# One pair's rotated keys taken from TensorE to GpSimd and DMAs, and the next pair's keys split before its queries, in an attention and mixture-of-experts kernel

## The chip, the cores and the metric

The kernel runs on one core of one Trainium2 chip. The metric is the device time of one execution in microseconds (us); of several runs the median is taken.

## What is computed

Attention with rotary embeddings over 4 batches, 8 heads, 576 tokens and a head width of 64, followed by a mixture of experts with one expert per token. The experts take most of the time after about 290 us and aren't touched here. The part that matters, cut:

```python
def rotate(x):
    x1, x2 = (x[..., :half], x[..., half:])
    return np.concatenate([x1 * cos - x2 * sin, x1 * sin + x2 * cos], axis=-1)
q_rot, k_rot = (rotate(q), rotate(k))
scores = scale * np.matmul(q_rot, k_rot.transpose(0, 1, 3, 2))
scores = scores - np.max(scores, axis=-1, keepdims=True)
attn = np.exp(scores)
attn = attn / (np.sum(attn, axis=-1, keepdims=True) + 1e-09)
return np.matmul(attn, v).astype(np.float32)
...
logits = np.einsum('bsd,de->bse', x, w_gate)
...
h = np.maximum(x[b, s] @ w1[e], 0.0)
out[b, s] = p[e] * (h @ w2[e])
```

## The kernel before

Two heads make a pair; there are 16 pairs, numbered from 0. A pair is nine tiles of 128 query rows against 576 keys (eight of one head each, and a tail tile of both heads' last 64 rows), so attention is 144 steps, g = 0 to 143. Up to g = 126 the order on every engine is the order of the code (a manual schedule).

Every number that goes through TensorE is a high part (fp32r) and the rest. In step g VectorE has the minimum mn of tile g (`softmax_min`, L278; the scores are negated, so the minimum is the maximum); TensorE makes the scores s of tile g+1 (`mm_s`, L273); ScalarE makes the exponentials e of tile g (`softmax_exp`, L295); VectorE takes the minimum of g+1; TensorE turns tile g-2 (`tr_main`, tm, L332), ScalarE copies it as its high part pth (`split_to`, L310) and VectorE makes the rest ptl (L314). Every fourth tile adds the narrow pieces tk, pkh, pkl. From g = 11 on the products with v follow (`pv_mm`, L371), ten steps behind. The scores have two PSUM buffers (pool ps_s): s of tile g+1 waits for the exponentials of tile g-1.

A pair's rotated queries and keys come in three ways.

- The usual way, from pair 2 on: SP loads four 128x576 pieces (queries, queries of the other half, keys, keys of the other half); GpSimd multiplies them by the table `tab` and adds two and two into `rr` (`rope_half`, L200 and L201), and splits rr into high part and rest in xq or xk (`split_qk`, L212 and L213). SP then spreads these with SBUF-to-SBUF DMAs: the tail queries (`spread_tail`, 2 DMAs), the queries (`spread_q`, 4) and the keys (`spread_k`, 6, to a tile m of the pool m_p, which has two buffers).
- Pair 0 (`first_pair`): VectorE and GpSimd make products with the table, and TensorE multiplies them by a 0/1 matrix `sel` (`turned`, L1144), which adds the two halves and puts them into both halves of the rows. ScalarE takes the high part from PSUM, VectorE the rest.
- Pair 1: the same, with products on GpSimd into the tile `raw`. `pair_1` (L1219) lists eight pieces: four `half_keys` of 288 columns (L1152 on ScalarE, L1155 on VectorE) and four `queries` of 256 or 320 columns (L1178 and L1184). The table START (L1246) puts them behind the steps 3 to 7.

The first index of `raw` holds pair 1's four pieces, the second pair 2's, which GpSimd turns at L200 and L201 in `rope_2` (step 3). The pool pt_p has four buffers: raw, then pth and ptl of pair 0 and pth of pair 1; ptl of pair 1 takes raw's place. The host lays out pairs 0 and 1 for the way with `sel` (`_laid_out`, L1402).

Queues: SP issues nearly all DMAs in the order of the code; one that waits holds up those behind it. A DMA of SP or ScalarE also waits for the landing of the eighth one before it. Pair p's spread is issued at the first step of pair p-1 (L1303), behind it the next loads of queries and keys (L1319); GpSimd's splits stand at step 5 (L1325).

Of the kernel before, what the change touches and what calls it, by code (L numbers as in the profile page):

```python
# [10 lines left out]
F32 = mybir.dt.float32  # L11
F32R = mybir.dt.float32r
# [5 lines left out]
ALU = mybir.AluOpType  # L18
# [119 lines left out]
def tile_attention_moe(ctx, tc, qk, v, tabs, turn, consts, tri, wg, wts, out):  # L138
# [48 lines left out]
    def load_qk(p):  # L187
        for f in (1, 0):
            load_half(p, f)
# [19 lines left out]
    def split_qk(p):  # L209
        parts = [(xq, rr)] if p % 2 == 0 else [(xk[1], rr[:, 1]), (xq[:, :, 0], rr[:, 0])]  # L210
        for x, src in parts:
            pool.tensor_scalar(x[:, 0], src, 1.0, 1.0, op0=ALU.mult, op1=ALU.mult)  # L212
            pool.tensor_tensor(x[:, 1], src, x[:, 0].bitcast(F32), op=ALU.subtract)  # L213

    def split_v(p):
        v2 = v2_p.tile([P, 10, 2, D], F32R, tag="v2", name=f"v2_{p}")
        src = vl[p % 2]
        pool.tensor_scalar(v2[:, :, 0], src, 1.0, 1.0, op0=ALU.mult, op1=ALU.mult)
        pool.tensor_tensor(v2[:, :, 1], src, v2[:, :, 0].bitcast(F32), op=ALU.subtract)
        v2_t[p] = v2  # L220
# [890 lines left out]
    def first_pair():  # L1111
        nonlocal qtail0

        wake = pk_p.tile([P, S], F32R, tag="pk", name="wake").bitcast(BF16)[:, 0:512]
        sel = et_p.tile([P, S], F32, tag="et", name="turn")[:, 0:P]
        sp.dma_start(qkl[:, 2, 0:HALF], qk[0, 0, :, 2, 0:HALF])
        act.dma_start(tab[:, 2, 0:HALF], tabs[:, 2, 0:HALF])
        sp.dma_start(qkl[:, 2, HALF:], qk[0, 0, :, 2, HALF:])
        act.dma_start(tab[:, 2, HALF:], tabs[:, 2, HALF:])
        act.dma_start(sel, turn)  # L1120
        sp.dma_start(qkl[:, 0, 0:256], qk[0, 0, :, 0, 0:256])
        sp.dma_start(qkl[:, 3], qk[0, 0, :, 3])
        sp.dma_start(qkl[:, 1, 0:256], qk[0, 0, :, 1, 0:256])
        for x in range(2):
            sp.dma_start(qkl[:, x, 256:], qk[0, 0, :, x, 256:])
        m_t[0] = m_p.tile([P, 2, 2, S], F32R, tag="m", name="m_0")
        qtail0 = et_p.tile([P, S], F32R, tag="et", name="qtail0")[:, 0:4 * P].rearrange("p (n a s) -> p n a s", n=2, a=2)
        qtail0 = [qtail0[:, n] for n in range(2)]


        dve.memset(wake, 0.0)
        awake = ps_t.tile([P, 512], F32, tag="t", name="wake_ps")

        def keep_awake(n):
# [11 lines left out]
        def half_keys(a, h, p=1, wait=False):

            ps = ps_t.tile([P, 512], F32, tag="t", name=f"k{p}_{a}_{h}")
            for c, lo, n in (((0, 0, HALF),), ((0, HALF, HALF),), ((64, 0, 224), (0, 512, 64)), ((0, 224, HALF),))[2 * a + h]:
                turned(2 + a, ps[:, c:c + n], lo, n, raw[:, 0] if p else qkl)  # L1150
            hi, lo = (m_t[p][:, a, c, h * HALF:(h + 1) * HALF] for c in range(2))
            act.copy(hi, ps[:, 0:HALF])  # L1152

            def rest():
                dve.tensor_tensor(lo, ps[:, 0:HALF], hi.bitcast(F32), op=ALU.subtract)  # L1155

            return rest if wait else rest()

        def keys(a):
            ps = ps_s.tile([P, 2, 512], F32, tag="s", name=f"k_{a}")  # L1160
            for h, c, lo, n in (((0, 0, 0, HALF), (1, 0, HALF, HALF)), ((0, 64, 0, 224), (1, 0, 224, HALF), (0, 0, 512, 64)))[a]:
                turned(2 + a, ps[:, h, c:c + n], lo, n)
            hi, lo = (m_t[0][:, a, c].rearrange("p (h s) -> p h s", h=2) for c in range(2))
            act.copy(hi, ps[:, :, 0:HALF])

            def rest():
                dve.tensor_tensor(lo, ps[:, :, 0:HALF], hi.bitcast(F32), op=ALU.subtract)

            return rest

        def queries(a, lo, hi, p=0):
            ps = ps_t.tile([P, 512], F32, tag="t", name=f"q{p}_{a}_{lo}")
            turned(a, ps[:, 0:hi - lo], lo, hi - lo, raw[:, 0] if p else qkl)
            parts = []
            for c0, c1 in ((lo, min(hi, 512)), (512, hi)):
# [24 lines left out]
        for x in (2, 3, 0, 1):  # L1200
            sp.dma_start(raw[:, 0, x], qk[0, 1, :, x])
        for x in range(2):
            products(x, 256, S, pool)
        low_k = keys(0)
        products(0, 0, 256)
        keep_awake(1)
        products(3)
        products(1, 0, 256)
        low_k()
        queries(0, 0, 256)()  # L1210
        second = [half_keys(1, h, 0, True) for h in range(2)]
        second.append(queries(1, 0, 256))
        mm_s(0)
        for f in second[0:2]:
            f()
        for x in (2, 3, 0, 1):
            products(x, engine=pool, of=raw[:, 0])
        m_t[1] = m_p.tile([P, 2, 2, S], F32R, tag="m", name="m_1")
        pair_1 = [lambda a=a, h=h: half_keys(a, h) for a in range(2) for h in range(2)]  # L1219
        pair_1 += [lambda a=a, lo=lo, hi=hi: queries(a, lo, hi, 1)() for a in range(2) for lo, hi in ((0, 256), (256, S))]  # L1220
        return [second[2], lambda: queries(0, 256, S)(), lambda: queries(1, 256, S)()], keep_awake, pair_1

    if True:
# [4 lines left out]
            rest_q, keep_awake, pair_1 = first_pair()  # L1228
        sp.dma_start(wid, wg)
        load_v(0)  # L1230
        sp.dma_start(tab[:, 3], tabs[:, 3])
        sp.dma_start(raw[:, 1], qk[0, 2])
        sp.dma_start(tab[:, 0:2], tabs[:, 0:2])
        load_v(1)
# [3 lines left out]
        sp.dma_start(rows_d[0:1], zrow)  # L1238

        def rope_2():  # L1240
            for f in (1, 0):
                rope_half(pool, f, raw[:, 1, 2 * f:2 * f + 2])

        NSTEP = NPAIR * 9
        soon, todo, minima = [], [], {}
        START = {  # L1246
            0: [lambda: split_v(0)], 1: [rest_q[1], lambda: keep_awake(1)], 2: [rest_q[2], lambda: load_qk(3)],
            3: [pair_1[0], pair_1[1], rope_2, lambda: split_qk(2)], 4: [pair_1[2]], 5: pair_1[3:5],
            6: pair_1[5:6], 7: pair_1[6:8] + [lambda: split_v(1), lambda: load_v(2)],
            8: [lambda: spread(2)], 40: [lambda: act.copy(trib, trif)],  # L1250
        }


# [146 lines left out]


def _laid_out(q, k, v, moe_w_gate, moe_w_local, moe_w1, moe_w2):  # L1402
    def turned(x):
        t = x.reshape(B, NP, 2, S, 2, D // 2).transpose(0, 1, 2, 4, 5, 3)
        x = np.stack([t.reshape(B, NP, 2, D, S), t[:, :, :, ::-1].reshape(B, NP, 2, D, S)], axis=4)
        x[:, :, 1] = x[:, :, 1, :, ::-1].copy()

        for hp in range(2):
# [5 lines left out]
    qk = np.concatenate([turned(q), turned(k)], axis=3)  # L1414
# [40 lines left out]
```

## Time and profile before

| | us |
|---|---|
| median of 3 runs | 538.61 |
| the 3 runs | 536.79, 538.71, 538.61 |
| the profiled execution | 537.63 |
| its span in the profile | 535.7 |
| TensorE busy (PE) | 515.3 |
| VectorE busy (DVE) | 377.4 |
| ScalarE busy (ACT) | 345.3 |
| GpSimd busy (POOL) | 346.1 |

In the profile an engine's work is named by the line of the kernel, the operation, and the tiles written and read (out<-in). Times are us from the start of the span. SPq is SyncE's queue, on which DMAs are issued. "[1.08 <-DVE gm L470]" behind a row says how long the engine had been idle and what ended that. The table is of the whole span; what a change in one stretch is worth has to be read from that stretch.

### The profile page before, as it was taken

Reading aid. Unit: us, or ns where it says so; the run is one execution under the profiler, and the core shown is the slowest. Engines: PE = TensorE matmul, PEld = TensorE weight load, DVE = VectorE, ACT = ScalarE, POOL = GpSimd, SP = SyncE. Lnnn points to the kernel's source line nnn. Section 1 sums busy time; section 2 is a strip of 40 time slices with the busy share of each in tenths; the row PEclk is TensorE's granted clock in tenths of the full one; section 3 lists DMA queues with packets and bytes.
Section 4 is the critical chain, followed back from the end, with each engine's and each line's share of the span. In section 5 each row is a group of like instructions: output and inputs, shape, how many; then the busy total and the mean of one; then the engine's idle time right before and its main releaser. Section 6 shows DMA issues by size and latency. Waiting matters only on the chain.

```text
span 535.7 us, 10815 instructions
## 1 busy us (share of the span) xinstructions
PE 515.3 (96%) x3273; PEld 458.9 (86%) x3273; DVE 377.4 (70%) x690; ACT 345.3 (64%) x766; POOL 346.1 (65%) x290
## 2 busy tenths in 40 slices
PE   7989999999999999999999899999999999999992
PEld 4889999999999999998978688887888888888881
DVE  6999999999999999999998746446421745411540
ACT  3988999999999999998877323252533344523440
POOL 4999999999999999983898202255412554411331
PEclk9999999999999999999999999999999999999997
DMA  8658788988879878866167214653446586537440
GB/s 280 275 133 224 224 221 232 236 188 215 221 224 246 200 194 211 239 150 159 24 210 227 65 55 142 190 205 127 169 105 231 150 325 182 181 90 235 107 151 25
DMA packets 65481, 97.33 MB, mean 182 GB/s; under 512 B 28353, under 2 KB 39105, under 8 KB 65282
## 3 DMA queue, kind: packets, MB, share of 16 engines
q1 hardware_dynamic: 61938, 86.45, 57.1%
q0 software_dynamic: 3040, 9.71, 5.6%
q8 instruction: 28, 0.46, 0.4%
q14 instruction: 43, 0.35, 0.3%
q10 hardware_dynamic: 432, 0.36, 0.2%
HBM read 76.95 MB, written 12.86 MB: 168 GB/s over the span
## 4 chain that ended last, share of the span: by engine, by line
PE 80%; DVE 8%; issue 4%; ACT 3%; POOL 2%; DMA 1%; ACTq 0%; POOLq 0%; DVEq 0%
PE h L981 19%; PE o L1024 17%; PE pv L371 14%; PE s L273 13%; PE tm L332 9%; PE gx L457 3%; DVE mn L278 2%; PE th L1015 2%; DVE ptl L314 2%; PE tx L967 2%; ACT e L295 1%; PE tk L342 1%; DMA turn<-in_turn_dram 1%; ACT pth L310 1%; DVE w L926 1%
## 5 line engine op out<-in xcount | busy, mean ns | idle before, releaser
L1024 PE MATMUL o<-w,hs 128*128 128x512 f32 x456 | 113.1, 398 | 0.0
L278 DVE TENSOR_REDUCE mn<-s 128x1 f32<-128x576 f32 x144 | 107.1, 743 | 2.3 <-PE s L273 1.1
L981 PE MATMUL h<-w,xs 128*128 128x512 f32 x444 | 106.4, 393 | 1.3 <-DVE xs L314 1.0
L295 ACT ACTIVATE e<-s,mn 128x576 f32<-128x576 f32 x128 | 95.5, 746 | 15.2 <-DVE mn L278 12.6
L1030 POOL DMA_INDIRECT out_dram<-os,sidx x19 | 23.1, 1213 | 125.4 <-ACTq L932 83.7
L314 DVE TENSOR_TENSOR ptl<-tm,pth 128x512 fp32r<-128x512 f32 x139 | 95.4, 687 | 11.5 <-ACT pth L310 8.8
L273 PE MATMUL s<-m,qst 128*128 128x288 f32 x512 | 96.2, 310 | 4.1 <-ACT e L295 3.0
L981 PEld LDWEIGHTS h<-w,xs 128*128 128x128 f32 x444 | 82.5, 188 | 19.9 <-DVE w L926 1.5
L1024 PEld LDWEIGHTS o<-w,hs 128*128 128x128 f32 x456 | 83.1, 188 | 17.0 <-DVE hs L314 0.4
L310 ACT CAST pth<-tm 128x512 fp32r<-128x512 f32 x139 | 80.7, 581 | 6.8 <-PE tm L332 6.2
L273 PEld LDWEIGHTS s<-m,qst 128*128 128x128 f32 x512 | 74.1, 188 | 9.0 <-ACT e L295 5.1
L371 PE MATMUL pv<-pth,v 128*128 128x288 f32 x256 | 76.8, 315 | 0.6 <-DVE ptl L314 0.4
L332 PE MATMUL tm<-wid,e 128*128 128x128 f32 x512 | 77.1, 272 | 0.0
L371 PE MATMUL pv<-ptl,v 128*128 128x288 f32 x256 | 76.5, 314 | 0.2 <-POOL ptl L307 0.2
L200 POOL TENSOR_TENSOR stage<-stage 128x1152 f32<-128x1152 f32 x26 | 69.4, 2669 | 1.1 <-DMA stage<-in_qk_dram 1.1
L332 PEld LDWEIGHTS tm<-wid,e 128*128 128x128 f32 x512 | 62.1, 140 | 0.8 <-DVE ptl L314 0.4
L926 DVE TENSOR_TENSOR w<-stage,w 128x1024 fp32r<-128x1024 f32 x37 | 51.2, 1418 | 14.6 <-ACT w L923 9.7
L371 PEld LDWEIGHTS pv<-pth,v 128*128 128x128 f32 x256 | 48.3, 189 | 2.0 <-DVE ptl L314 0.7
L371 PEld LDWEIGHTS pv<-ptl,v 128*128 128x128 f32 x256 | 48.3, 189 | 0.5 <-POOL ptl L307 0.4
L314 DVE TENSOR_TENSOR xs<-tx,xs 128x512 fp32r<-128x512 f32 x19 | 13.1, 688 | 44.9 <-ACTq L932 35.0
L201 POOL TENSOR_TENSOR stage<-stage 128x576 f32<-128x576 f32 x26 | 37.1, 1427 | 2.0
L314 DVE TENSOR_TENSOR hs<-th,hs 128x512 fp32r<-128x512 f32 x26 | 17.4, 687 | 28.1 <-ACTq L932 16.6
(202 smaller groups left out, 821.7 us busy)
## 6 DMA issues: line engine op xcount, KB each, us to landing
stage<-in_wts_dram SPq DMA_DIRECT2D x84, 512.0 KB
stage<-in_qk_dram SPq DMA_DIRECT2D x26, 576.0 KB
qst<-xq SPq DMA_DIRECT2D x56, 128.0 KB
stage<-in_v_dram SPq DMA_DIRECT2D x16, 320.0 KB
m<-xq SPq DMA_DIRECT2D x14, 288.0 KB
m<-xk SPq DMA_DIRECT2D x14, 288.0 KB
m<-xq SPq DMA_DIRECT2D x14, 256.0 KB
m<-xk SPq DMA_DIRECT2D x14, 256.0 KB
```

The source lines that it names most:

```text
L200: engine.tensor_tensor(x, x, tab[:, 2 * f:2 * f + 2], op=ALU.mult)
L201: engine.tensor_tensor(rr[:, f], x[:, 0], x[:, 1], op=ALU.add)
L273: pe.matmul(st[:, h, lo:hi], lhs, keys[:, k0:k0 + hi - lo], start=(n == 0), stop=(n == len(parts_) - 1))
L278: dve.tensor_reduce(mn, s_t[g][:, :, 0:HALF], axis=AX.XY, op=ALU.min)
L295: act.activation(dst.rearrange("p (h s) -> p h s", h=2), s_t.pop(g)[:, :, 0:HALF], AF.Exp, bias=mn, scale=-1.0, accum_out=sums[:, col:col ...
L310: act.copy(hi, src)
L314: dve.tensor_tensor(lo, src, hi.bitcast(F32), op=ALU.subtract)
L332: pe.transpose(ps[:, k], src[:, k * P:(k + 1) * P], ident)
L371: pe.matmul(pv_t[p, u], lhs.rearrange("p c d -> p (c d)"), rhs, start=(n == 0), stop=(n == 9))
L926: (pool if k in on_pool else dve).tensor_tensor(lo, src, hi.bitcast(F32), op=ALU.subtract)
L981: pe.matmul(ps[:, c], xs_t[t][:, x, k], w[y][:, c * 512:(c + 1) * 512], start=(k == 0 and n == 0), stop=(k == 3 and n == 2))
L1024: pe.matmul(ps, hs_t[t][:, x, k], w[y][:, (k % 2) * 512:(k % 2 + 1) * 512], start=(k == 0 and n == 0), stop=(k == 7 and n == 2))
```

## The change

Pair 1's keys are now made the usual way: GpSimd adds the two key products into rr and splits them into xk, and SP spreads them with six DMAs (`spread_k(1)`, step 2). GpSimd therefore takes one query product, the two key products, their sum, the split, and the other query product, and the four raw loads and one piece of the table are issued in another order. The four `half_keys` pieces of pair 1 are gone. Its queries come in two pieces of 512 columns and one of both heads' 64 tail columns, at the steps 3, 6 and 7. Pair 2's keys are summed and split (`rope_2` with `split_half`) before its queries are multiplied, and spread at step 7; its tail and its queries are spread at step 8. The host lays out pair 1's keys as those of later pairs.

```diff
+            split_half(x, src)
+
+    def split_half(x, src):
+        pool.tensor_scalar(x[:, 0], src, 1.0, 1.0, op0=ALU.mult, op1=ALU.mult)
+        pool.tensor_tensor(x[:, 1], src, x[:, 0].bitcast(F32), op=ALU.subtract)
...
-        for x in (2, 3, 0, 1):
+        for x in (0, 2, 3, 1):
+            if x == 3:
+                sp.dma_start(tab[:, 3], tabs[:, 3])
             sp.dma_start(raw[:, 0, x], qk[0, 1, :, x])
...
-        for x in (2, 3, 0, 1):
-            products(x, engine=pool, of=raw[:, 0])
-        m_t[1] = m_p.tile([P, 2, 2, S], F32R, tag="m", name="m_1")
-        pair_1 = [lambda a=a, h=h: half_keys(a, h) for a in range(2) for h in range(2)]
-        pair_1 += [lambda a=a, lo=lo, hi=hi: queries(a, lo, hi, 1)() for a in range(2) for lo, hi in ((0, 256), (256, S))]
+        products(0, engine=pool, of=raw[:, 0])
+        for x in range(2):
+            pool.tensor_tensor(raw[:, 0, 2 + x], raw[:, 0, 2 + x], tab[:, 2 + x], op=ALU.mult)
+        pool.tensor_tensor(rr[:, 1], raw[:, 0, 2], raw[:, 0, 3], op=ALU.add)
+        split_half(xk[1], rr[:, 1])
+        products(1, engine=pool, of=raw[:, 0])
+
+        def queries_1(a):
+            ps = ps_t.tile([P, 512], F32, tag="t", name=f"q1_{a}")
+            turned(a, ps, 0, 512, raw[:, 0])
+            return scaled(qst[1][:, a], ps)
+
+        def tails_1():
+            ps = ps_t.tile([P, 512], F32, tag="t", name="q1_tail")
+            for a in range(2):
+                turned(a, ps[:, 64 * a:64 * a + 64], 512, 64, raw[:, 0])
+            dst = qtail0[1].rearrange("p a (c s) -> p (a c) s", c=2)[:, 0:4:3]
+            return scaled(dst, ps[:, 0:P].rearrange("p (a s) -> p a s", a=2))
+
+        def scaled(dst, src):
+            act.activation(dst, src, AF.Copy, scale=-0.125)
+            low = slice(64, 128)
+            dve.scalar_tensor_tensor(dst[low], src[low], -0.125, dst[low].bitcast(F32), op0=ALU.mult, op1=ALU.subtract)
+
+        pair_1 = [lambda: queries_1(0), lambda: queries_1(1), tails_1]
...
-        sp.dma_start(tab[:, 3], tabs[:, 3])
...
         def rope_2():
-            for f in (1, 0):
+            for f, x in ((1, xk[0]), (0, xq[:, :, 0])):
                 rope_half(pool, f, raw[:, 1, 2 * f:2 * f + 2])
+                split_half(x, rr[:, f])
+
+        def spread_2():
+            spread_tail(2)
+            spread_q(2)
...
-            0: [lambda: split_v(0)], 1: [rest_q[1], lambda: keep_awake(1)], 2: [rest_q[2], lambda: load_qk(3)],
-            3: [pair_1[0], pair_1[1], rope_2, lambda: split_qk(2)], 4: [pair_1[2]], 5: pair_1[3:5],
-            6: pair_1[5:6], 7: pair_1[6:8] + [lambda: split_v(1), lambda: load_v(2)],
-            8: [lambda: spread(2)], 40: [lambda: act.copy(trib, trif)],
+            0: [lambda: split_v(0)], 1: [rest_q[1], lambda: keep_awake(1)], 2: [rest_q[2], lambda: spread_k(1), lambda: load_qk(3)],
+            3: [rope_2, pair_1[0]], 6: pair_1[1:2],
+            7: pair_1[2:3] + [lambda: split_v(1), lambda: spread_k(2), lambda: load_v(2)],
+            8: [spread_2], 40: [lambda: act.copy(trib, trif)],
```

How this moves instructions, at three places. GpSimd, from pair 1's products to pair 2's split, before (raw's products, then v, then both sums of pair 2 and one split xq of 1152 columns):

```order
L1141 TENSOR_TENSOR raw<-raw,stage 128x576 x4
L218 TENSOR_SCALAR v_0_228<-stage 128x10x64
L219 TENSOR_TENSOR v_0_228<-stage,v_0_228 128x10x64
L200 TENSOR_TENSOR raw<-raw,stage 128x1152
L201 TENSOR_TENSOR stage<-raw 128x576
L200 TENSOR_TENSOR raw<-raw,stage 128x1152
L201 TENSOR_TENSOR stage<-raw 128x576
L212 TENSOR_SCALAR xq<-stage 128x1152
L213 TENSOR_TENSOR xq<-stage,xq 128x1152
```

and in the change, up to the first half of pair 2 (the second half follows with four more of the same kinds):

```order
L1144 TENSOR_TENSOR raw<-raw,stage 128x576
L1223 TENSOR_TENSOR raw<-raw,stage 128x576 x2
L1224 TENSOR_TENSOR stage<-raw 128x576
L215 TENSOR_SCALAR xk_101<-stage 128x576
L216 TENSOR_TENSOR xk_101<-stage,xk_101 128x576
L1144 TENSOR_TENSOR raw<-raw,stage 128x576
L221 TENSOR_SCALAR v_0_230<-stage 128x10x64
L222 TENSOR_TENSOR v_0_230<-stage,v_0_230 128x10x64
L200 TENSOR_TENSOR raw<-raw,stage 128x1152
L201 TENSOR_TENSOR stage<-raw 128x576
L215 TENSOR_SCALAR xq<-stage 128x576
L216 TENSOR_TENSOR xq<-stage,xq 128x576
```

The key sum and the key split of pair 1 (L1224, L215, L216) are new on GpSimd and stand ahead of everything else; pair 2's split is in two.

VectorE, from the step that takes pair 1's first pieces to the first query piece, before (m is pair 1's keys, k and q are PSUM tiles):

```order
L1155 TENSOR_TENSOR m_201<-k_0_0_298,m_201 128x288
L1155 TENSOR_TENSOR m_201<-k_0_1_302,m_201 128x288
L278 TENSOR_REDUCE mn_322<-s_315 128x1
L314 TENSOR_TENSOR ptl_262<-tm_324,pth_261 128x4x128
L1155 TENSOR_TENSOR m_201<-k_1_0_331,m_201 128x288
L278 TENSOR_REDUCE mn_345<-s_339 128x1
L314 TENSOR_TENSOR ptl_262<-tm_347,pth_261 128x4x128
L314 TENSOR_TENSOR pkl_264<-tk_354,pkh_263 128x256
L1155 TENSOR_TENSOR m_201<-k_1_1_359,m_201 128x288
L1184 SCALAR_TENSOR_TENSOR qst_100<-q_0_0_363,qst_100 64x256
L278 TENSOR_REDUCE mn_377<-s_370 128x1
```

and in the change, over the same tiles:

```order
L1243 SCALAR_TENSOR_TENSOR qst_100<-q_0_315,qst_100 64x512
L281 TENSOR_REDUCE mn_329<-s_322 128x1
L317 TENSOR_TENSOR ptl_264<-tm_331,pth_263 128x4x128
L281 TENSOR_REDUCE mn_347<-s_341 128x1
L317 TENSOR_TENSOR ptl_264<-tm_349,pth_263 128x4x128
L317 TENSOR_TENSOR pkl_266<-tk_356,pkh_265 128x256
L281 TENSOR_REDUCE mn_371<-s_364 128x1
```

Four key pieces and a query piece are gone from among the minima, and one query piece of 512 columns stands ahead of them.

SP's queue behind the loads of the start, in the change (m_280 is pair 1's key tile, m_416 pair 2's):

```order
L1262 DMA rows_d<-ohr 1x513
L230 DMA m_280<-xk_101 64x1152
L231 DMA m_280<-xk_101 64x2x512
L232 DMA m_280<-xk_101 64x2x64
L230 DMA m_280<-xk_101 64x1152
L231 DMA m_280<-xk_101 64x2x512
L232 DMA m_280<-xk_101 64x2x64
L193 DMA stage<-in_qk_dram 128x1152 x2
L230 DMA m_416<-xq 64x2x576
```

Before, the two loads of pair 3 (L193) followed the first row directly; now pair 1's six spreads stand between, and behind the loads come pair 2's key spreads, ahead of its tail and queries.

## Rows read from the trace of the kernel before

**Rows 1.** The page: the chain that ended last, shares of the span by engine.

```profile
PE 80%; DVE 8%; issue 4%; ACT 3%; POOL 2%; DMA 1%; ACTq 0%; POOLq 0%; DVEq 0%
```

**Rows 2.** Windows: stretch, length, busy us (instructions) of PE, PEld, DVE, ACT, POOL, clock, DMA share, GB/s.

```profile
15.00:30.00 15.00, 13.52 (x90) 11.79 (x89) 14.54 (x29) 13.19 (x36) 14.53 (x9) 1.00 0.51 201
```

**Rows 3.** Timeline of VectorE: start, length, engine, line, operation, tiles.

```profile
16.88 0.76 DVE L278 TENSOR_REDUCE mn<-s 128x1 f32<-128x576 f32 x1
...
27.71 0.76 DVE L278 TENSOR_REDUCE mn<-s 128x1 f32<-128x576 f32 x1
...
29.11 0.75 DVE L278 TENSOR_REDUCE mn<-s 128x1 f32<-128x576 f32 x1
...
33.51 0.69 DVE L314 TENSOR_TENSOR ptl<-tm,pth 128x512 fp32r<-128x512 f32 x1
...
244.05 0.27 DVE L526 TENSOR_REDUCE mx<-lg_all 128x15 f32<-128x120 f32 x1
```

**Rows 4.** Timeline of GpSimd, the same columns.

```profile
7.50 1.68 POOL L1141 TENSOR_TENSOR stage<-stage 128x320 f32<-128x320 f32 x2 [7.05 <-DMA stage<-in_qk_dram]
9.15 5.53 POOL L1141 TENSOR_TENSOR raw<-raw,stage 128x576 f32<-128x576 f32 x4
...
25.34 1.16 POOL L212 TENSOR_SCALAR xq<-stage 128x1152 fp32r<-128x1152 f32 x1
...
29.20 0.74 POOL L218 TENSOR_SCALAR v<-stage 128x640 fp32r<-128x640 f32 x1
...
38.41 1.42 POOL L201 TENSOR_TENSOR stage<-stage 128x576 f32<-128x576 f32 x1
39.79 0.68 POOL L212 TENSOR_SCALAR xk<-stage 128x576 fp32r<-128x576 f32 x1
...
41.96 0.68 POOL L212 TENSOR_SCALAR xq<-stage 128x576 fp32r<-128x576 f32 x1
...
221.99 2.66 POOL L200 TENSOR_TENSOR stage<-stage 128x1152 f32<-128x1152 f32 x1 [0.86 <-DMA stage<-in_qk_dram]
...
239.20 0.57 POOL L502 TENSOR_TENSOR gm<-gm 128x180 f32<-128x180 f32 x1 [1.08 <-DVE gm L470]
...
240.62 0.09 POOL L505 MEMSET lg_all<- 1x1 f32 x1
```

**Rows 5.** GpSimd's waits, 30 to 240 us: us in total, times, longest.

```profile
POOL stage L200 <- DMA stage<-in_qk_dram: 1.1, 2, 0.9
```

**Rows 6.** Groups by form, 14 to 31 us: count, busy us, mean ns, idle before.

```profile
L314 DVE TENSOR_TENSOR ptl<-tm,pth 128x512 fp32r<-128x512 f32 x8 | 5.5, 687 | 0.2
...
L1184 DVE SCALAR_TENSOR_TENSOR qst<-q,qst 64x256 fp32r<-64x256 f32 x6 | 2.5, 426 | 0.4 <-ACT qtail L1178 0.3
...
L1155 DVE TENSOR_TENSOR m<-k,m 128x288 fp32r<-128x288 f32 x4 | 1.7, 446 | 0.0
...
L1184 DVE SCALAR_TENSOR_TENSOR qtail<-q,qtail 64x64 fp32r<-64x64 f32 x4 | 0.9, 221 | 0.0
```

**Rows 7.** Timeline of TensorE, tiles of scores.

```profile
22.82 1.56 PE L273 MATMUL s<-m,qtail 128*128 128x288 f32 x10
...
27.35 0.76 PE L273 MATMUL s<-m,qst 128*128 128x288 f32 x4 [0.53 <-DVE qst L1184]
...
59.99 0.79 PE L273 MATMUL s<-m,qst 128*128 128x288 f32 x4
```

**Rows 8.** Timeline of SP's queue: issue, time to issue, line, tiles.

```profile
3.98 0.81 SPq L1125 DMA_DIRECT2D stage<-in_qk_dram  x2
...
44.17 1.28 SPq L240 DMA_DIRECT2D qtail<-xq  x2
...
48.08 0.59 SPq L227 DMA_DIRECT2D m<-xk  x1
...
50.26 1.15 SPq L227 DMA_DIRECT2D m<-xk  x1
...
217.37 1.64 SPq L193 DMA_DIRECT2D stage<-in_qk_dram  x2
```

More of the change, by code (lines that the diff above doesn't have):

```diff
@@ L211, in split_qk @@
         for x, src in parts:
-            pool.tensor_scalar(x[:, 0], src, 1.0, 1.0, op0=ALU.mult, op1=ALU.mult)
-            pool.tensor_tensor(x[:, 1], src, x[:, 0].bitcast(F32), op=ALU.subtract)
+            split_half(x, src)
+    def split_half(x, src):
+        pool.tensor_scalar(x[:, 0], src, 1.0, 1.0, op0=ALU.mult, op1=ALU.mult)
+        pool.tensor_tensor(x[:, 1], src, x[:, 0].bitcast(F32), op=ALU.subtract)
     def split_v(p):
@@ L1144, in turned, with half_keys @@
             pe.matmul(dst, sel, of[:, x, lo:lo + n], start=True, stop=True)
[L1146 to L1151, printed above, removed]
+        def half_keys(h):
+            ps = ps_t.tile([P, 512], F32, tag="t", name=f"k_1_{h}")
+            for c, lo, n in (((64, 0, 224), (0, 512, 64)), ((0, 224, HALF),))[h]:
+                turned(3, ps[:, c:c + n], lo, n)
+            hi, lo = (m_t[0][:, 1, c, h * HALF:(h + 1) * HALF] for c in range(2))
             act.copy(hi, ps[:, 0:HALF])
@@ L1155, in rest @@
                 dve.tensor_tensor(lo, ps[:, 0:HALF], hi.bitcast(F32), op=ALU.subtract)
-            return rest if wait else rest()
+            return rest
         def keys(a):
@@ L1169, in keys, with queries @@
             return rest
-        def queries(a, lo, hi, p=0):
-            ps = ps_t.tile([P, 512], F32, tag="t", name=f"q{p}_{a}_{lo}")
-            turned(a, ps[:, 0:hi - lo], lo, hi - lo, raw[:, 0] if p else qkl)
+        def queries(a, lo, hi):
+            ps = ps_t.tile([P, 512], F32, tag="t", name=f"q_{a}_{lo}")
+            turned(a, ps[:, 0:hi - lo], lo, hi - lo)
             parts = []
@@ L1176, in queries @@
                 if c1 > c0:
-                    dst, src = qtail0[p][:, a, 64 * a:64 * a + 64] if c0 == 512 else qst[p][:, a, c0:c1], ps[:, c0 - lo:c1 - lo]
+                    dst, src = qtail0[0][:, a, 64 * a:64 * a + 64] if c0 == 512 else qst[0][:, a, c0:c1], ps[:, c0 - lo:c1 - lo]
                     act.activation(dst, src, AF.Copy, scale=-0.125)
@@ L1210, in first_pair @@
         queries(0, 0, 256)()
-        second = [half_keys(1, h, 0, True) for h in range(2)]
+        second = [half_keys(h) for h in range(2)]
         second.append(queries(1, 0, 256))
@@ L1402, in _laid_out, with turned @@
 def _laid_out(q, k, v, moe_w_gate, moe_w_local, moe_w1, moe_w2):
-    def turned(x):
+    def turned(x, own):
         t = x.reshape(B, NP, 2, S, 2, D // 2).transpose(0, 1, 2, 4, 5, 3)
@@ L1406, in turned @@
         x[:, :, 1] = x[:, :, 1, :, ::-1].copy()
-        for hp in range(2):
+        for hp in range(own):
             y = x[0, hp].copy()
@@ L1412, in turned @@
         return x.reshape(B, NP, P, 2, S)
-    qk = np.concatenate([turned(q), turned(k)], axis=3)
+    qk = np.concatenate([turned(q, 2), turned(k, 1)], axis=3)
     vp = v.reshape(B, NP, 2, S, D)
```

## The prediction

> **What bounds the kernel now.** I read the chain of waits first, then the windows, then single engines in order of time. TensorE holds 80% of the chain [rows 1]: whatever moves an early stage moves the end by as much, so long as nothing in between waits. The window of 15 to 30 us [rows 2] shows where TensorE is not the limit: it is busy for 13.52 us, VectorE for 14.54 and GpSimd for 14.53, at a granted clock of 1.00. The change edits just this stretch. Between VectorE's minimum at 16.88 and the one at 29.11 [rows 3] lie six tiles, 12.23 us, with pair 1's pieces among them; two minima with only one ptl between them stand 1.40 us apart (27.71 and 29.11).
>
> GpSimd is the second thing to see. Its first wait ends at 7.50 us [rows 4]; from 30 to 240 us it waits twice for a load, 1.1 us together [rows 5], and once for VectorE, 1.08 us at 239.20 [rows 4]. It works almost without a pause for 230 us, so what it loses early it doesn't win back. Nobody waits for it today only because its results are early.
>
> **What goes.** VectorE loses four key pieces of 446 ns, four query pieces of 426 and two of 221 [rows 6]: 3.93 us. It gains two query pieces of 64x512, priced by the ptl row, also 512 columns, at 687, and one of 64x2x64, taken as 290, between the 221 and the 426: 1.66 us. Net 2.27 us off the engine that paces this stretch. ScalarE drops a piece for each of the ten and gets three; TensorE drops the ten-instruction block of k products and keeps its query columns. Both had idle time left, so they give nothing beyond VectorE's 2.27.
>
> Not all of it arrives. Six plain tiles of 1.40, plus one pkl piece, 256 columns wide like a query piece of 0.43, and the 1.66 added, are 10.49 us, 1.74 less than 12.23. Besides, the tail tile at 22.82 takes TensorE 1.56 us, where the next tile takes 0.76 [rows 7]; today the crowded VectorE hides that, afterwards I count half of the extra 0.80 as open. **Taken: 1.4 us**, with 1.0 and 2.27 as ends.
>
> **What GpSimd gets.** Its four products stay. New are one sum (38.41 to 39.79 in the row of a later pair: 1.38 us) and one key split (39.79 to 41.96: 2.17); pair 2's split of 3.86 (25.34 to 29.20) becomes two halves of 2.17 [rows 4]: 1.38 + 2.17 + 0.48 = 4.03 us. It may also wait for raw 3 or for the table piece, now the fourth and the third of these loads. In the old run four loads of this size, issued at the same place, were all in use by 13.3, where the fourth product began (9.15 + 3 x 1.38) without a wait. The product that needs them now stands at 9.15 + 2 x 1.38 = 11.91, so the wait lies between 0 and 1.4; I take 0.2, since GpSimd never waited for any of the four. **GpSimd is then 4.2 us late** (4.0 to 5.4), and stays late. Who meets that, in order:
>
> *Pair 1's keys.* The split ends at 9.15 + 4 x 1.38 + 2.17 + 0.2 = 17.0. By the spacing of pair 3's spread (48.08 to 50.26 for three transfers [rows 8]) the fourth goes out 2.2 us later, the sixth after 4.4: 19.2 and 21.4. No row gives a spread's landing. The nearest are two loads that GpSimd waited for: issued at 3.98, used at 7.50 (3.5 us), and issued at 217.37, used at 221.99 (4.6 us) [rows 4, 8]. So the second tile's keys are there at 24.9 to 26.0. TensorE asked at 27.35 [rows 7], now about 1.0 earlier, at 26.3. No wait taken; a late drain of the loads ahead of it could cost 0.5.
>
> *The buffer of raw.* The first ptl of pair 1 takes its place. GpSimd had read it for the last time by 25.34; a key sum, a key split and half of pair 2's split now come before that, 1.38 + 2.17 + 2.17 + 0.2 = 5.9: 31.2. VectorE wrote that ptl at 33.51 [rows 3], now at 32.1. No wait, 0.9 us of room.
>
> *Pair 2.* Its queries are split 4.2 us later, but no longer stand behind its keys on SP, whose six spreads take 4.4. So they go out no later than now.
>
> *Pair 3's keys, the tightest place.* SP began this spread at 44.17, straight behind GpSimd's split (41.96 + 2.17 = 44.13), issued the fourth m transfer at 50.26, and TensorE used it at 59.99 [rows 4, 7, 8]. With a landing of 3.5 to 4.6 the reserve is 5.1 to 6.2 us. The lateness eats 4.2, which leaves 0.9 to 2.0 for TensorE to come earlier. The middle, 1.4, is what the stretch gives; I take 0.2 off for the lower half of that span. Later pairs meet the same lateness, but it is a fixed shift, and from there TensorE and GpSimd both advance at their old pace.
>
> *The routing.* GpSimd stood ready at 238.12 (239.20 less its wait of 1.08) and ended its score sums at 240.71; VectorE read them at 244.05 [rows 3, 4]. The load wait of 0.86 before 221.99 dissolves, so GpSimd comes 3.3 late, ready at 241.5, and ends at 243.0; VectorE, 1.2 early, asks at 242.85. That is 0.1 us, or up to 1.3 with the late end.
>
> The loads of pair 3 on SP now stand behind pair 1's spreads, until about 22 us. GpSimd wants them after its v split, at 29.20 and 4.2 later, so they cost nothing. Pair 1's queries are turned three tiles later than the keys were; their products are done by then (17.0 + 1.4). The moved table load delays raw 3 and 1 by one place, which is in the wait above.
>
> **Sum.** 1.4 off the stretch, 0.2 given back at pair 3: 1.2 us. Against the profiled execution, 537.63 us (span 535.7 and 1.9 around it), that is 536.4. The median of the three runs, 538.61, stands 0.98 above that execution, so for a median the prediction is **537.4 us**. The three runs lie 1.9 us apart, and 0.5% of 538.61, about what a measurement of this kernel can tell from no change, is 2.7 us: more than the whole 2.27 that VectorE sheds. I forecast no change that counts.
>
> For the landing of one spread the Trainium skill has a price (DMA: Bandwidth & Descriptors, section on the anatomy of one DMA): about 2.0 us fixed and the bytes at 436 GB/s, stated for GpSimd's queue, which as an estimate is 2.7 us for 288 KB. By it pair 3 would have 7.0 us of reserve and the 0.2 would not be given back; no run here shows it.
>
> **Rivals.** *All that VectorE sheds arrives.* For it: VectorE is idle for only 0.5 us from 15 to 30 us [rows 2]. Against it: the 1.40 between plain minima. It also needs landings near 3.5 us, so that pair 3 leaves 2.0. 538.61 - 2.27 = 536.3.
>
> *GpSimd's lateness decides, and the kernel is slower.* For it: 230 us almost without a pause, and a reserve at pair 3 that may be as small as 5.1 us. It decides once the lateness passes the reserve. With both bad ends, 5.4 against 5.1, TensorE comes to pair 3's keys at 60.3 instead of 59.99; the 1.4 is gone and 0.3 with it: 538.9. For over 0.5% the lateness would have to reach 5.1 + 2.7 = 7.8 us, almost twice what the rows add up to; only something unseen, such as slower GpSimd work beside the new transfers, gives that. One key split's subtraction takes VectorE 446 ns for 288 columns [rows 6], 0.89 for 576, and GpSimd some 1.4 of the 2.17. The Trainium skill (GPSIMD Engine Reference, Engine selection) advises VectorE for elementwise work and calls GpSimd about twice as slow with two inputs; the rows agree roughly, with 1.6, and that rule speaks for this rival.
>
> *It does nothing.* With the full 1.4 of a wait and the late landing, pair 1's sixth transfer is there at 21.4 + 1.2 + 4.6 = 27.2, and TensorE starts the second tile at its old 27.35 less 0.15. 538.5.
>
> **How the numbers follow.** Forecast 0.58 (its own range 536.7 to 538.2), all of it arrives 0.18, slower through GpSimd 0.16, nothing 0.08. The first rival goes below 535.9, the 0.5% mark, only with some of the runs' own spread: 0.12 for faster. Half of the GpSimd rival, 0.08, is what no row bounds: slower by over 0.5%. The rest, 0.80, is within it. The range runs from 535.8, the full 2.27 and half a us of spread, to 539.3, the GpSimd case with as much.
>
> **What would show it.** Right: VectorE's minima of 16.88 and 29.11 some 10.8 us apart instead of 12.23; pair 1's split ending near 17.0; TensorE at pair 3's first m tile near 58.8 instead of 59.99, after a short wait or none; GpSimd without pauses to about 241. Wrong: TensorE waiting for a transfer at 25 to 27, or for over 1 us at about 60; VectorE's first ptl of pair 1 waiting for GpSimd; a stretch that shrinks by over 2.3 us.

## The result: slower by 0.56%, and the profile after

The changed kernel takes 540.14 us (median of 10 runs, 538.88 to 542.07) where the kernel before, beside it, takes 537.34 (10 runs, 535.68 to 538.71): ratio 1.0056, 95% interval 1.0042 to 1.0070. Its profiled execution took 540.54, its span 538.8. I had forecast no change that counts, 1.2 us less than before; against the median of the ten runs it is 2.80 more.

Four more rows of the kernel before are needed (timelines: start, length, engine, line, operation, tiles; the first is pair 3's tail tile, the last a tail tile near the end of attention):

```profile
58.11 0.96 PE L273 MATMUL s<-xk,qtail 128*128 128x288 f32 x6
...
62.13 0.79 PE L273 MATMUL s<-m,qst 128*128 128x288 f32 x4
...
79.20 0.41 DVE L471 TENSOR_TENSOR xrow<-gx,sum 128x256 f32<-128x256 f32 x1
...
239.91 0.96 PE L273 MATMUL s<-xq,qtail 128*128 128x288 f32 x6
```

The changed kernel, TensorE's tiles of scores:

```profile
25.54 0.76 PE L276 MATMUL s<-m,qst 128*128 128x288 f32 x4 [0.81 <-DMA m<-xk]
26.49 0.78 PE L276 MATMUL s<-m,qst 128*128 128x288 f32 x4
...
56.86 0.96 PE L276 MATMUL s<-xk,qtail 128*128 128x288 f32 x6
61.13 1.28 PE L276 MATMUL s<-m,qst 128*128 128x288 f32 x4 [2.12 <-ACT et L298]
64.81 0.78 PE L276 MATMUL s<-m,qst 128*128 128x288 f32 x4
...
242.94 0.95 PE L276 MATMUL s<-xq,qtail 128*128 128x288 f32 x6
```

The stretch gave what was hoped: pair 3's tail tile starts at 56.86 instead of 58.11, 1.25 us earlier. The next tile, pair 3's first with m, comes at 61.13 instead of 59.99 [rows 7], the one after it at 64.81 instead of 62.13: 2.68 late. Near the end TensorE is 3.03 late, which is the loss.

VectorE, and the windows (length, busy us and instructions of PE, PEld, DVE, ACT, POOL, granted clock, DMA share, GB/s):

```profile
16.68 0.76 DVE L281 TENSOR_REDUCE mn<-s 128x1 f32<-128x576 f32 x1
...
28.00 0.75 DVE L281 TENSOR_REDUCE mn<-s 128x1 f32<-128x576 f32 x1
...
62.45 0.76 DVE L281 TENSOR_REDUCE mn<-s 128x1 f32<-128x576 f32 x1 [2.66 <-PE s L276]
...
82.51 0.42 DVE L474 TENSOR_TENSOR xrow<-gx,sum 128x256 f32<-128x256 f32 x1 [0.56 <-DMA rows_d<-xrow]
```

```profile
15.00:30.00 15.00, 12.58 (x86) 10.55 (x85) 13.92 (x24) 12.48 (x32) 14.50 (x11) 1.00 0.85 265
...
60.00:62.00 2.00, 0.87 (x4) 0.90 (x4) 0.00 (x0) 0.30 (x2) 1.92 (x2) 0.79 0.91 286
62.00:64.00 2.00, 2.00 (x10) 1.98 (x10) 0.84 (x2) 0.70 (x2) 2.00 (x2) 0.50 1.00 386
64.00:66.00 2.00, 2.00 (x16) 2.00 (x16) 1.50 (x4) 0.81 (x3) 2.00 (x1) 0.86 0.36 113
```

The minima that stood 12.23 us apart [rows 3] stand 11.32 apart. VectorE's busy time from 15 to 30 falls from 14.54 [rows 2] to 13.92. Behind the gap at 60 TensorE's granted clock is 0.50 (1.2 GHz) from 62 to 64 and whole again after 66; VectorE has nothing to do for 2.66 us. The last VectorE row is a place that the prediction did not name: the row block xrow, whose buffer is not free until a store of rows_d has landed.

GpSimd and SP's queue:

```profile
9.89 1.42 POOL L1144 TENSOR_TENSOR raw<-raw,stage 128x576 f32<-128x576 f32 x1 [0.27 <-DMA raw<-in_qk_dram]
...
47.82 1.44 POOL L216 TENSOR_TENSOR xq<-stage,xq 128x576 fp32r<-128x576 f32 x1
```

```profile
49.28 1.30 SPq L243 DMA_DIRECT2D qtail<-xq  x2
50.67 2.48 SPq L238 DMA_DIRECT2D qst<-xq  x4
53.20 0.59 SPq L230 DMA_DIRECT2D m<-xk  x1
...
55.35 1.16 SPq L230 DMA_DIRECT2D m<-xk  x1
...
72.84 1.56 SPq L193 DMA_DIRECT2D stage<-in_qk_dram  x2
74.50 0.38 SPq L484 DMA_DIRECT2D rows_d<-xrow  x1
74.93 0.52 SPq L488 DMA_DIRECT2D rows_d<-xrow  x1
75.55 0.54 SPq L484 DMA_DIRECT2D rows_d<-xrow  x1
```

Pair 3's spread begins at 49.28 instead of 44.17, 5.1 us late, and its fourth key transfer goes out at 55.35 instead of 50.26 [rows 8]. The profile puts TensorE's wait down to the exponentials et, whose last row on ScalarE ends at 60.30, 0.8 before TensorE starts. The trace also keeps every count of the DMAs' semaphores; I call the last count of a DMA its landing. The fourth key transfer landed at 60.93, just before TensorE starts, and in keys_first below the tile does not wait for et at all. The stores of rows_d stand behind a spread that waits for GpSimd, and behind two loads: VectorE's own block was made at 65.22, and its two stores go out at 74.50 and 74.93.

### The profile page after: what moved, and what is told of

Same layout as the page of the kernel before. It is cut to its first block, busy times and chain, and to the rows that moved or that the text cites. A ratio compares the mean times of both kernels' runs of the same rounds, so it can differ in the third digit from the quotient of the medians.

```text
span 538.8 us, 10796 instructions
## 1 busy us (share of the span) xinstructions
PE 515.3 (96%) x3263; PEld 458.7 (85%) x3263; DVE 377.1 (70%) x683; ACT 343.8 (64%) x759; POOL 350.1 (65%) x295
## 5 line engine op out<-in xcount | busy, mean ns | idle before, releaser
L1027 PE MATMUL o<-w,hs 128*128 128x512 f32 x456 | 113.2, 398 | 0.0
L1027 PEld LDWEIGHTS o<-w,hs 128*128 128x128 f32 x456 | 83.0, 188 | 17.2 <-DVE hs L317 0.4
```

The lines of the kernel that those rows point to most:

```text
L1027: pe.matmul(ps, hs_t[t][:, x, k], w[y][:, (k % 2) * 512:(k % 2 + 1) * 512], start=(k == 0 and n == 0), stop=(k == 7 and n == 2))
```

## Experiments

All ratios are to the kernel before, run beside it; a line of "..." stands for what is left out. A door is a place where an engine waits for something that GpSimd's lateness has delayed; it is open where the engine does not wait. "First door" is pair 3's keys near 60 us, "second door" VectorE's wait for a store near 80.

**keys_first**: pair 3's keys ahead of its queries.

```diff
-                if i == 0 and ours:
+                if i == 0 and p == 2:
+                    spread_k(3)
+                    spread_tail(3)
+                    spread_q(3)
+                elif i == 0 and ours:
```

> Theory L (GpSimd is late): the changed kernel loses its time because pair 3's key transfers go out some 5 us later than before; the first m tile of pair 3 started on TensorE at 61.13 us, where 58.7 was due. Here SP issues pair 3's six key transfers as soon as the key split ends (about 47.1 in the changed kernel), ahead of the queries, which wait for the query split (49.2). By L the fourth key transfer goes out near 49.4 instead of 55.35, TensorE starts that tile near 58.7 without a wait, the granted clock stays 1.00, and the time is that of before less the 1.25 us of the stretch, plus up to 0.4 that goes elsewhere (at 82 to 85 us): 536.1 to 536.5 where before has 537.34. Rival E (what the profile names for this wait, the exponentials of the tail tile, is what TensorE waits for): nothing moves, 61.1 and 540.1. Rival Q: the queries, now behind six transfers, become the wait: the first m tile starts later than 59.

Measured: 541.03 us, 1.0062 [1.0039, 1.0086]. TensorE's row and the exponentials et, then SP's stores, VectorE's wait, TensorE's behind it, and a window:

```profile
58.98 0.79 PE L276 MATMUL s<-m,qst 128*128 128x288 f32 x4
...
59.70 0.75 ACT L298 ACTIVATE et<-s,mn 128x576 f32<-128x576 f32 x1
```

```profile
74.71 0.38 SPq L484 DMA_DIRECT2D rows_d<-xrow  x1
75.14 0.52 SPq L488 DMA_DIRECT2D rows_d<-xrow  x1
75.75 0.54 SPq L484 DMA_DIRECT2D rows_d<-xrow  x1
...
81.82 0.42 DVE L474 TENSOR_TENSOR xrow<-gx,sum 128x256 f32<-128x256 f32 x1 [3.57 <-DMA rows_d<-xrow]
...
82.39 0.63 PE L335 MATMUL tm<-wid,et 128*128 128x128 f32 x4 [2.22 <-DVE xrow L474]
```

```profile
75.00:90.00 15.00, 12.15 (x82) 11.53 (x81) 9.76 (x21) 9.62 (x27) 14.52 (x13) 0.89 1.00 237
```

The first wait was the key transfers: it is gone, the tile starts ahead of et, and the clock stays up. The time is not better, because VectorE now stands 3.57 us at the second door, TensorE waits 2.22 us for it, and there the clock falls (0.89 on average from 75 to 90 us). The wait of the changed kernel had only paid for that in advance. The store that VectorE waits for is that of its own block of pair 0: its instruction waits for the semaphores of the stores at 74.71 and 75.14, which landed at 81.26 and 81.73. The store of GpSimd's block, at 75.75, landed at 83.40, when VectorE had gone on.

**less_2_7** and **less_5_3**: GpSimd relieved of pair 2's products with the table, of the keys (less_2_7) or of both (less_5_3, whose edit is shown).

```diff
-                rope_half(pool, f, raw[:, 1, 2 * f:2 * f + 2])
+                pool.tensor_tensor(rr[:, f], raw[:, 1, 2 * f], raw[:, 1, 2 * f + 1], op=ALU.add)
```

> Left out of the computation: pair 2's keys are not multiplied by the table (one GpSimd product of 2.67 us less); all else as in the changed kernel. Theory L: GpSimd is then 2.4 us late instead of 5.1, the fourth key transfer of pair 3 goes out near 52.7 and lands by 56.8 to 58.3, before TensorE comes at 58.7: no wait, no fall of the clock, 536.1 to 536.5. Rival C (the key transfers of pair 3 got slower through the change itself, the lateness only moves them): a wait of about 1 us or more and half of the loss stay, 538 to 539.5.

Measured: 537.44, 1.0000 [0.9984, 1.0015]. The results are wrong, but the expert phase keeps its 456 matmuls, so the time can be compared. No wait at 59; at the second door:

```profile
79.19 0.42 DVE L474 TENSOR_TENSOR xrow<-gx,sum 128x256 f32<-128x256 f32 x1 [1.02 <-DMA rows_d<-xrow]
```

The wait ends at 79.19 instead of 81.82 in keys_first: 2.63 earlier for 2.67 us of GpSimd work taken away. In this pair of runs what ends it follows GpSimd one to one. It also ate most of the gain, since 79.19 is where VectorE stood before.

> Left out of the computation: pair 2's queries and keys are not multiplied by the table (two GpSimd products of 2.67 us less); all else as in the changed kernel. GpSimd is then no later than before (5.1 - 5.3 = -0.2). Theory S: no wait at pair 3 nor at the store near 78 us, the whole 1.25 us of the stretch arrives: 535.9, ratio 0.9977. In less_2_7, with 2.4 us of lateness, a wait of 1.02 for the store had eaten it. Rival (the 1.25 is lost behind the stretch whatever GpSimd does): 537.1.

Measured: 630.47. The scores are others, tokens go to other experts and the expert phase has 528 matmuls at L1027 instead of 456, so only its trace up to 240 us counts. It shows no wait at either door, and the late tail tile at 239.38 instead of 239.91; it began its stretch 0.3 us later than before. With GpSimd in time the gain that it had at pair 3 (tail tile at 57.60 instead of 58.11) reaches the end of attention.

**awake**: TensorE kept busy in the gap.

```diff
+        if g == 28:
+            for _ in range(30):
+                pe.matmul(st[:, 0, 0:P], onesb, onesb, start=True, stop=True)
```

> The changed kernel, with thirty bf16 matmuls of 128 columns on TensorE just ahead of pair 3's first m tile, in the gap in which it waits (their result is overwritten). Theory K: of the 2.7 us that the changed kernel had lost by 66.8 against before, the wait itself is 2.4 less the 1.25 gained, and about 1.5 is the lower clock after the gap (granted 0.50 from 62 to 64). Then with the engine kept busy the granted clock stays 1.00, the wait is as long as before (61.1), and the time falls by about 1.5 us, to 538.6. Rival R (what is lost behind the wait is the chain of minimum, exponentials and turn that has to fill again): the clock may stay up, but the time remains near 540.1.

Measured: 539.91, 1.0055 [1.0036, 1.0075].

```profile
59.32 1.84 PE L265 MATMUL s<-onesb 128*128 128x128 bf16 x30
60.97 0.78 PE L279 MATMUL s<-m,qst 128*128 128x288 f32 x4
63.09 0.79 PE L279 MATMUL s<-m,qst 128*128 128x288 f32 x4
```

```profile
62.00:64.00 2.00, 2.00 (x18) 2.00 (x17) 1.70 (x5) 1.51 (x4) 1.90 (x2) 1.00 0.99 397
```

Theory K is right about the clock: it stays 1.00, and the next tile comes 2.12 us after the first instead of 3.68, so the lower clock cost 1.56. It does not repeat the wait: here the fourth key transfer landed at 59.44, and it is the thirty matmuls that hold the tile until 60.97. But the time stays: the wait at the second door is 1.44 here, 0.9 more than in the changed kernel.

**before_late4** and **before_late4b**: lateness alone, in the kernel before. Four more sums on GpSimd, ahead of pair 2's split or (b) behind it.

```diff
+                for _ in range(2):
+                    pool.tensor_tensor(rr[:, f], raw[:, 1, 2 * f], raw[:, 1, 2 * f + 1], op=ALU.add)
```

> The kernel before, with each of pair 2's two sums on GpSimd made three times (four more operations of 1.38 us, the same results): 5.5 us of lateness without anything else of the change. Pair 3's fourth key transfer should go out at 50.26 + 5.5 = 55.8. Theory L, lateness alone: if it takes the 5.6 us that TensorE's start in the changed kernel points to, TensorE starts pair 3's first m tile near 61.3 instead of 59.99, with a fall of the clock behind it, and the kernel is 1.5 to 3 us slower than before. Rival C (those transfers are slow only through the change itself): they take the 4.1 us or so that fit before, TensorE starts at 60.0 and the time is that of before within 0.4.

Measured: 544.26, 1.0120 [1.0097, 1.0144]. Neither theory named the place:

```profile
47.85 1.30 PE L273 MATMUL s<-m,qst 128*128 128x288 f32 x4 [4.85 <-DMA qst<-xq]
```

In the old order pair 2's queries are spread behind its one split. In the kernel before the last of them landed at 40.70 and the tile started at 43.56, 2.9 us later; here the spread begins 6.6 us late (35.86 for 29.28). The change takes that place away by splitting and spreading keys and queries apart: they land by 39.90 and are used at 42.30.

> The kernel before, with pair 2's two sums on GpSimd made two times more each, but behind pair 2's split (four operations of 1.38 us, the same results): 5.5 us of lateness from pair 1's v split on, without the shorter stretch and without pair 2's queries being late, which cost before_late4 its 4.85 us. Theory S: pair 3's fourth key transfer is there between 59.9 and 61.3, VectorE's store near 79.2 waits about 3 us (in the old kernel it would have had some 2.5 of room), and TensorE is about 3 us late from 85 us on as in the changed kernel: 539.9 to 541 beside 536.9 for before. Rival P (the loss of the changed kernel comes from its new transfers of pair 1 or its other order, not from GpSimd's lateness): under 538.

Measured: 541.01, 1.0090 [1.0075, 1.0106].

```profile
35.42 0.69 DVE L314 TENSOR_TENSOR ptl<-tm,pth 128x512 fp32r<-128x512 f32 x1 [2.13 <-POOL stage L1247]
...
82.77 0.42 DVE L471 TENSOR_TENSOR xrow<-gx,sum 128x256 f32<-128x256 f32 x1 [1.63 <-DMA rows_d<-xrow]
```

The wait at 35.42 is of my own making, since the added sums read raw to the end. It has TensorE 1.7 late at pair 3's tail tile already, and GpSimd's split of pair 3 ends 6.1 late. But without any of the change's transfers, VectorE passes the second door at 82.77, as the changed kernel does at 82.51, and TensorE is 3.4 late near 240. Rival P falls.

**stores_first** and **keys_stores** (with pair 3's keys first): the stores ahead of the loads.

```diff
-                    if p + 3 < NPAIR:
+                    if p + 3 < NPAIR and not ours:
...
                     soon.pop(0)()
+                if i == 0 and ours and p + 3 < NPAIR:
+                    load_qk(p + 3)
```

> The changed kernel with only the second of the two edits: the stores of rows_d ahead of the loads on SP; pair 3's transfers as in the changed kernel. Theory S: pair 3's wait and the fall of the clock behind it stay (2.7 us late at 66.8), the 0.4 at 82 us vanishes: 539.8 beside 537.1 for before, so alone it saves almost nothing, as keys_first alone saved nothing. Rival (the store is the only door that counts): the time falls below 538.5.

> The changed kernel with pair 3's key transfers issued ahead of its queries (as in keys_first) and with each pair's three stores of rows_d issued ahead of its two loads of queries and keys on SP, instead of behind them. Theory S, formed from keys_first: GpSimd's lateness of 5 us reaches TensorE by two doors, pair 3's keys near 61 us and, some 20 us later, VectorE's wait for a store of rows_d (3.57 us in keys_first), because SP issues those stores behind a spread that waits for GpSimd and behind two loads of 576 KB. With both doors open the 1.25 us of the stretch arrive: no wait at 59 or at 78, 535.9 to 536.6 beside 537.1 for before. Rival T (a third door: pair 5's keys near 92, or the routing near 240 us, which can take up to 1.3): 537 to 539.5. Rival D (the loads, now later, make GpSimd wait and later still): GpSimd shows load waits from 70 us on and the time is 538 or more.

Measured: 548.43, 1.0226 [1.0201, 1.0252], and 548.12, 1.0201 [1.0181, 1.0222]. GpSimd's waits from 14 to 240 us in stores_first, and a window:

```profile
POOL stage L200 <- DMA stage<-in_qk_dram: 10.8, 8, 2.7
```

```profile
240.00:270.00 30.00, 24.41 (x185) 22.28 (x184) 25.47 (x52) 20.83 (x52) 22.63 (x33) 1.00 0.63 137
```

Rival D came true: the loads land late, GpSimd waits for them 10.8 us in all and the spread behind it is later still (stores_first's own second door is open, at 79.12); at 240 to 270 TensorE is busy for 24.41 us, where it was 28.15 before.

**queries_only**: the kernel before with pair 1's queries in 512 columns.

```diff
-        pair_1 += [lambda a=a, lo=lo, hi=hi: queries(a, lo, hi, 1)() for a in range(2) for lo, hi in ((0, 256), (256, S))]
+        pair_1 += [lambda: queries_1(0), lambda: queries_1(1), tails_1]
```

> The kernel before with one part of the change alone: pair 1's queries in two pieces of 512 columns and one of tails instead of four of 256 and 320; its keys are made on TensorE as before, GpSimd does what it did. VectorE sheds 4 x 426 + 2 x 221 ns and gains two pieces near 690 and one near 290: 0.48 us net. If VectorE paces the stretch, its minima of 16.88 and 29.11 move together by 0.2 to 0.5 us and the time is 536.6 to 536.9 beside 537.1, too little for the runs to tell from nothing. GpSimd and the store near 78 us show no change. Rival: the broader pieces hold up the minimum of a tile (a piece of 690 ns sits in front of it), and the stretch does not shrink or grows.

Measured: 537.22, 1.0010 [0.9994, 1.0026]. VectorE's minima over the same six tiles:

```profile
16.44 0.76 DVE L278 TENSOR_REDUCE mn<-s 128x1 f32<-128x576 f32 x1
...
28.45 0.74 DVE L278 TENSOR_REDUCE mn<-s 128x1 f32<-128x576 f32 x1
```

12.01 us instead of 12.23: 0.22, at the low end, and below what the runs resolve.

**keys_halves**, **keys_rows**, **keys_halves_rows**: pair 3's keys first, with the stores between the two loads (only the load of the queries moved behind them), with row blocks moved to VectorE, and with both. The row blocks:

```diff
-            if j0 == 0 and p < POOL_ROWS:
+            if j0 == 0 and 2 <= p < POOL_ROWS:
```

> The changed kernel with pair 3's key transfers ahead of its queries, as in keys_first, and with the stores of rows_d between the two loads on SP: the load of the keys, for which GpSimd waited in keys_stores and stores_first, keeps its place, and only the load of the queries goes behind the stores (GpSimd wants it some 5 us later). By theory S the store lands 1.5 to 2 us earlier, VectorE's wait of 3.57 in keys_first falls to some 1.5 to 2, GpSimd shows no wait for a load, and the time is 538 to 539 beside 536.9. Rival D2 (any place ahead of a load makes GpSimd wait again): 541 or more.

> The changed kernel with pair 3's key transfers ahead of its queries, and with the first three row blocks of pairs 0 and 1 made by VectorE (from PSUM) instead of GpSimd, which saves GpSimd 1.2 us for each: lateness 3.9 from 68 us on and 2.7 from 84 us. Theory S: the wait for the store near 78 falls from 3.57 to about 2.4, if VectorE, which gets 0.7 us more work in a pair, doesn't pay for it elsewhere: 538.5 to 540 beside 536.9. Rival V (VectorE is as full as GpSimd): no better than keys_first, 540.5 or more.

> Both: the stores between the loads, and the row blocks of pairs 0 and 1 on VectorE, with pair 3's keys first. If the two reliefs add, the wait for the store near 78 falls to 0.5 or less, most of the 1.25 us of the stretch arrives, and the time is 536 to 537.5 beside 536.9. Rival: one door takes what the other gives, 538.5 or more.

Measured: 539.81, 1.0057 [1.0042, 1.0071]; 537.39, 1.0009 [0.9995, 1.0023]; 536.43, 1.0000 [0.9987, 1.0012]. The stores between the loads gave nothing: VectorE passes the second door at 82.12, and GpSimd waits 1.7 us for loads from 14 to 240. In keys_halves' profiled execution pair 1's keys also came late, 2.55 us, which is a third door:

```profile
26.80 1.30 PE L276 MATMUL s<-m,qst 128*128 128x288 f32 x4 [2.55 <-DMA m<-xk]
```

keys_rows opens the second door altogether, where I had expected 2.4 us of wait to stay:

```profile
78.81 0.42 DVE L474 TENSOR_TENSOR xrow<-gx,sum 128x256 f32<-128x256 f32 x1
```

```profile
60.89 0.39 SPq L484 DMA_DIRECT2D rows_d<-xrow  x1
```

GpSimd's split of pair 3 is as late as in keys_first, and the store of VectorE's own block of pair 0 goes out only 0.3 us earlier (74.38 for 74.71); it lands after VectorE has gone on. VectorE's instruction waits here for another semaphore, and of the stores on that one only the store at 60.89 had landed, at 64.83: that of pair 0's first three row blocks, which in keys_first are GpSimd's and go out at 75.75. So the moved blocks open the door because VectorE gets a buffer that is free 14 us before it is wanted, and not by 2.4 us of relief for GpSimd. Why the buffers go round differently the runs do not show.

**after_rows** and **before_rows**: the row blocks on VectorE alone, in the changed kernel and in the one before.

> The changed kernel with the row blocks of pairs 0 and 1 on VectorE alone; pair 3's transfers go out as in the changed kernel. This is the missing cell between keys_first (541.03, first door open), keys_rows (537.39, both open) and the changed kernel (540.14, none). Theory S (two doors, the later wait decides): no wait for the store near 80, but pair 3's wait near 61 and the fall of the clock stay, 2.7 us late from 66.8 on: 539 to 540.3 beside 536.9 for before. Rival O (the store near 80 is the only door that counts in the end, and pair 3's wait is made up for later): 537.5 or less, as keys_rows.

> The kernel before with the same row blocks of pairs 0 and 1 on VectorE: what this relief alone does where GpSimd is not late. VectorE gets some 0.7 us more in two pairs, GpSimd 1.2 us less in each; with no door shut TensorE can only lose: 0 to 0.6 us, 536.9 to 537.5. Rival W (GpSimd holds up the old kernel too, somewhere): faster by 0.5 us or more.

Measured: 537.94, 1.0021 [1.0006, 1.0036], and 537.31, 1.0008 [0.9995, 1.0021].

```profile
54.84 1.17 SPq L230 DMA_DIRECT2D m<-xk  x1
```

```profile
59.14 0.77 PE L276 MATMUL s<-m,qst 128*128 128x288 f32 x4
61.98 0.77 PE L276 MATMUL s<-m,qst 128*128 128x288 f32 x4 [0.46 <-DMA m<-xk]
```

In this execution pair 3's fourth key transfer landed 4.1 us after its issue and the first m tile did not wait; the next waited 0.46 for the rest. In stores_first and awake, where SP issues it at the same place, it landed after 4.1 and 4.3 us, in the changed kernel after 5.6. So the wait of 2.12 us is not in every execution: some 1.4 of it is that long landing. Nor does the loss hang on the fall of the clock: of the changed kernel's ten runs the five with the higher mean granted clock (0.993 to 0.996, where the kernel before has 0.992 to 0.997) have a median of 539.95 us, the other five (0.990 to 0.992) 540.54.

That gives the square:

| | GpSimd makes the row blocks | VectorE makes those of pairs 0 and 1 |
|---|---|---|
| pair 3's queries first | 1.0056 (changed kernel) | 1.0021 (after_rows) |
| pair 3's keys first | 1.0062 (keys_first) | 1.0009 (keys_rows) |

The second door makes 0.35% to 0.53%. What the first makes, 0.12% with the second open and nothing with it shut, is within the intervals and not resolved. No version beats the kernel before by what the runs can tell. The moved blocks cost something themselves: the tiles at 63.14 and 65.21 in keys_rows stand 2.07 us apart, in keys_first (63.06 and 64.90) 1.84, and before_rows is not faster than before.

## Why the prediction was wrong

**The stretch: right.** Minima 11.32 us apart (10.8 forecast), TensorE 1.25 earlier at pair 3 (1.4 taken, though 1.74 less half of 0.80 is 1.34; 1.0 the lower end). A part was lost at pair 1's keys, where I took no wait and kept 0.5. Their fourth transfer landed 5.3 us after its issue (19.99 to 25.29), where I had taken 3.5 to 4.6: a wait of 0.81 in the changed kernel, 2.55 in keys_halves.

**GpSimd's lateness: right.** 4.2 forecast, 4.0 to 5.4 its ends; 5.1 at pair 3's spread, 4.6 in after_rows. Of the 5.1, 0.74 is a first product at 9.89 instead of 9.15, which varies without the change too (9.87 in before_rows). Counted from the first product, pair 3's split ends 4.4 us later in the changed kernel, 4.3 to 4.8 in those made from it. One reading on the way was off: the ratio of 1.6 between GpSimd and VectorE doubles 446 ns, but VectorE's own subtraction of 576 columns (L1167 in the kernel before) takes 758 ns, and 1.44 is 1.9 times that.

**Raw's buffer, pair 2, the routing: no loss, as forecast.**

**Pair 3's keys: named, and priced too low.** I charged 0.2 us, with a landing of 3.5 to 4.6 taken from two loads. It was 4.1 in the kernel before, 4.1 to 4.3 in three kernels with the change and 5.6 in the changed kernel's profiled execution. The estimate of 2.7 from the Trainium skill (DMA: Bandwidth & Descriptors, the anatomy of one DMA), which I had not used, is further off. And where the clock falls, a wait costs more than its length: I had no term for the clock, 1.56 us there.

**The step that failed** is "Later pairs meet the same lateness, but it is a fixed shift". The list of those who meet it stopped at spreads and loads. SP's queue carries the stores of rows_d too, behind a spread that waits for GpSimd, and VectorE needs a landed store for its next row block. So the lateness is not a fixed shift for everybody: VectorE, which is early, meets it and stops. The reserve could have been read. In the kernel before, the store of VectorE's own block landed at 76.91 and VectorE came for a buffer at 79.20: 2.3 us, less than the 4.2 of lateness that I had. The time at which the second door opens hangs on GpSimd and hardly on TensorE:

| kernel | VectorE waits there | and passes | late tail tile |
|---|---|---|---|
| before | - | 79.20 | 239.91 |
| less_2_7 | 1.02 | 79.19 | 239.71 |
| awake | 1.44 | 81.68 | 242.16 |
| keys_first | 3.57 | 81.82 | 243.64 |
| keys_halves | 0.78 | 82.12 | 242.53 |
| changed kernel | 0.56 | 82.51 | 242.94 |
| before_late4b | 1.63 | 82.77 | 243.34 |

With pair 3's split 4.7 to 6.1 us late on GpSimd it opens at 81.7 to 82.8, 2.5 to 3.6 us after VectorE came in the kernel before, whatever TensorE had gained or lost ahead of it. So the rival "GpSimd's lateness decides" came true at a lateness of 5.1, not of 7.8: its bound counted pair 3's reserve alone.

**The range and the chances.** The range was hung on a median of three runs, 538.61, that lies 1.27 above the median of ten; by its own terms its upper end is 539.4, not 539.3. The result lies beyond either, and more than 0.5% slower is what had got a chance of 0.08.

## What to carry to other kernels

Where an engine without pauses gets late, follow its queue: list everything that stands behind its waits on the queue that issues DMAs, stores included, and for each the buffer that must come free, with the reserve from its landing to its next use. A wait that is taken away early can be standing in for a later one, so open the doors together (a square of two edits) before either is called the cause. And put nothing ahead of a load for which the late engine waits: here the loss became four times what it was.

## What was not expected of the hardware

- After 2.12 us without work TensorE's granted clock went from 1.00 to 0.50 and was back from 64.6 us on; thirty bf16 matmuls of 128 columns (1.84 us) in the gap kept it at 1.00. The fall cost 1.56 us, nearly as much as the gap.
- The same transfer of 64 rows between SBUF tiles, issued at the same place in the same order, landed 4.1 to 4.3 us after its issue in three executions (after_rows, stores_first, awake) and 5.6 in a fourth (the changed kernel).
- Stores of VectorE's block, 96 KB in two DMAs, behind two loads of 576 KB landed up to 7.5 us after their issue (74.93 to 82.42).
- Three stores ahead of two loads on SP made GpSimd wait 10.8 us for loads from 14 to 240 us, where it had waited 1.1 [rows 5].
